# Reversed quarters, a least-loaded order for the values, sketches that add up in PSUM, and a new task list

## The chip, the cores and the metric

The kernel runs on one core of a Trainium2 chip. The metric is the device time of the program in microseconds. A core has five engines with a queue each: TensorE (PE), VectorE (DVE), ScalarE (ACT), GpSimd (POOL) and SyncE (SP), which here issues nearly all DMAs. Each works through its own instructions in order and waits on semaphores for the others.

## The reference

Two blocks follow each other. Shapes: batch 4, heads 4, sequence 1088, head size 32; in the second block width 128, 4 experts of size 64, 2 chosen for each row.

```python
def phi(x):                      # x: q or k
    a = einsum('rd,bhsd->bhsr', S1, x)
    b = einsum('rd,bhsd->bhsr', S2, x)
    return einsum('bhsi,bhsj->bhsij', a, b).reshape(..., 64)
kv  = einsum('bhsf,bhsd->bhfd', phi(k), v);   z = sum(phi(k), axis=2)
x   = (phi(q) @ kv) / (phi(q) @ z + 1e-6)     # heads side by side: (4, 1088, 128)

logits = x @ w_gate;  topk = the 2 largest of 4;  w = softmax over them
for e in range(4):
    q, k, v = x @ wq[e], x @ wk[e], x @ wv[e]
    a  = causal softmax(q @ k.T / sqrt(64))
    out += (e is chosen) * w[e] * (a @ v @ wo[e])
```

S1 and S2 come as 64-bit floats; the kernel splits them into two 32-bit parts, a high and a low one (`NS = 2`). All matmuls that count here are in 32-bit floats, and each shows as two passes in the trace.

## The kernel before, in words

The four batches go through the same stages, one batch shifted against the next. A list of words in the source, `ORDER`, is the program: `1.ks:4:9` calls the task `ks` for batch 1 with the arguments 4 and 9, and every engine's queue gets its instructions in the order of the words. Nothing is scheduled by itself; a word stands in all the queues that it uses.

A batch has 1088 rows, which are 9 tiles of 128 (the last has 64). The words of a batch are:

- `ld` loads k, q and v (SP). `bk`, `bq` (`bq0`, `bq1` by halves for batch 0) turn k and q on VectorE (L319 to L326). `vk` brings the first batch's v into place.
- `ks`, `qs`: `sketch` (L333). Matmuls with SKW, the arranged S, give a and b for some tiles (L345), with the high and the low part of S side by side; ScalarE copies one (L350), VectorE adds the other (L352), and a product of a and b makes the 64 features (L355), on VectorE for batch 0, on GpSimd for the others.
- `kv` (L368) multiplies k's features and v; `tf` turns q's features (L280, copied by L281), `nu` forms numerators and denominators (L384) and divides (L388 to L391), giving `xs`; `tx` turns `xs` into `xT`. `sp` spreads `xs` to `xrep` by 16 DMAs (L271), which has one buffer.
- `em` and `eo` make the experts' matrices `mcat` (query and key weights multiplied) and `mo` (value and output weights).
- `ga`, `ge`, `gw`: the gate, a chain of small operations. `mp` (batch 0) and `md` make masks from it, `mk`, by matmuls and casts (L491, L494) or by a round trip of DMAs through DRAM (L475 to L482).
- `cu:i` (`chosen`): x times mcat for the tiles i and i+1 (L502). The two chosen experts' results are picked by the masks (L509) into `uT`.
- `s:i:j` (`scores`): scores of a tile against all keys up to it, for both chosen experts (L542, L563 for tile 8). VectorE adds the causal mask and takes the maximum (L517), ScalarE the exponentials with their sums (L521).
- `t:i` turns a tile's weights in blocks of 32 by 32 (L264). Tiles 1 to 5 are group B, tiles 0, 6, 7, 8 group A.
- `vb:p`, `va:p`: `values` (L575), in four parts for each group. The sums over keys run by chunks c of 32 keys. Each of the four quarters r of 32 partitions holds the queries 32r to 32r+31 of every tile of the group, has its own 32 rows of the array and its own PSUM bank, and needs the chunks up to c = 4i + r of tile i. So quarter 3 needs the most. The loops go over c and inside it over r (L585, L587), with one matmul for all the units (tile and chosen expert) that still need c:

```python
        last = {(i, r): min(4 * i + r, NC - 1) for i in tiles for r in range(4)}
        for c in range(*PARTS[grp][part : part + 2]):
            for r in range(4):
                us = [x for x, (i, s) in enumerate(units) if c <= last[i, r]]
```

- `shb`, `sha`, `shp`: the gate's weights over the sums, spread over partitions. `zb` multiplies them in and sorts the units by expert (L665 to L668). `o` multiplies by mo (L675), copies (L678, two buffers `ob`) and writes the output (L680).
- `warm:n` issues n matmuls that nobody reads.

PSUM has eight banks; a task takes the least recently used ones, and the value sums hold four banks for the time of their group.

Of the kernel before, what the change touches and what calls it, by code (L numbers as in the profile page):

```python
# [10 lines left out]
F32 = mybir.dt.float32  # L11
BF16 = mybir.dt.bfloat16
U8 = mybir.dt.uint8
F8 = mybir.dt.float8e4
I32 = mybir.dt.int32
ALU = mybir.AluOpType
# [6 lines left out]
    0.bk 0.ks:4:9 0.warm:2 0.bq1 0.ks:0:4 0.vk 0.kv 0.bq0 0.qs:0:4 0.qs:4:9 1.ld 1.bk 0.warm:2 0.tf:0:8 0.warm:2  # L23
    0.nu:0:4 0.tf:8:13 0.tf:13:18 1.ks:4:9 0.tx:0:4 1.ks:0:4 0.nu:4:9 0.ga:0:4 0.em 0.mp:2:4 0.ge:0 0.mp:0:2 1.bq
    0.tx:4:9 2.ld 0.cu:2 0.gw:0 1.kv 1.qs:4:9 0.ga:4:9 0.sp 1.qs:0:4 0.cu:0 0.eo 1.tf:8:13 0.mp:8:9 0.md 0.mp:6:8
    0.mp:4:6 1.tf:13:18 2.bk 0.s:3 0.t:3 0.cu:4 0.cu:6 0.cu:8 2.bq 3.ld 1.tf:0:8 2.ks:0:4 0.s:5:1 1.nu:0:5 2.ks:4:9
    0.t:5 0.s:4:2 0.t:1 1.nu:5:9 0.s:6:0 2.kv 1.tx:4:9 0.ge:4 1.tx:0:4 0.t:4 0.t:2 0.s:8 0.gw:4 0.shb 2.qs:0:4 0.vb:0
    0.vb:1 0.t:0 0.t:8 1.ga:0:9 1.ge:0 1.md 0.t:6 0.s:7 0.vb:2 0.vb:3 0.t:7 1.cu:0 2.qs:4:9 1.cu:6 1.cu:2 0.sha 1.cu:4
    0.va:0 0.zb:1 2.tf:0:8 3.bq 1.gw:0 0.va:1 0.va:2 3.bk 2.tf:8:13 0.va:3 0.zb:6 1.sp 2.tf:13:18 3.ks:4:9 1.s:5:1
    0.o:6 1.cu:8 1.t:1 1.t:5 0.o:1 0.zb:3 1.s:4:2 0.zb:0 1.t:2 0.o:3 2.nu:5:9 3.ks:0:4 2.nu:0:5 1.s:3 1.shb 0.zb:5  # L30
    0.o:0 2.tx:4:9 1.s:7 2.tx:0:4 3.kv 1.t:3 1.t:4 0.zb:8 3.qs:4:9 1.s:6:0 1.vb:0 2.ga:0:9 1.s:8 2.md 1.vb:1 1.t:7
    0.o:8 1.t:8 1.t:6 1.vb:2 2.ge:0 1.vb:3 2.gw:0 2.cu:4 3.tf:13:18 2.cu:8 2.cu:0 1.t:0 0.o:5 2.cu:2 2.s:5:1 3.tf:8:13
    2.t:5 1.sha 2.s:4:2 2.t:2 1.zb:3 1.va:0 1.va:1 1.va:2 3.qs:0:4 1.va:3 1.o:3 1.zb:6 2.t:1 1.zb:1 2.sp 2.cu:6
    3.tf:0:8 2.s:3 1.o:6 1.o:1 2.t:3 2.t:4 2.s:7 1.zb:0 2.s:6:0 3.nu:5:9 3.nu:0:5 2.t:6 1.zb:8 2.vb:0 2.shb 3.tx:4:9
    1.o:0 3.tx:0:4 1.zb:5 2.t:7 2.vb:1 1.o:8 3.ga:0:9 3.ge:0 3.md 2.t:0 2.vb:2 2.vb:3 2.zb:1 1.o:5 2.s:8 2.t:8 3.cu:6
    2.o:1 2.sha 3.cu:4 3.cu:0 3.cu:8 3.cu:2 3.s:5:1 3.t:1 3.s:4:2 3.t:2 3.s:3 2.va:0 2.va:1 2.zb:3 3.gw:0 3.t:5 3.t:3
    2.va:2 2.va:3 3.sp 3.t:4 2.zb:6 2.o:3 3.s:7 3.s:6:0 2.zb:0 3.s:8 2.o:6 2.o:0 3.vb:0 2.zb:5 2.o:5 2.zb:8 3.t:8
    3.shb 3.t:6 3.t:0 3.vb:1 3.vb:2 3.t:7 3.vb:3 3.va:0 3.va:1 3.shp 3.zb:3 3.va:2 2.o:8 3.zb:1 3.va:3 3.o:3 3.zb:6
    3.o:1 3.o:6 3.zb:8 3.o:8 3.zb:5 3.o:5 3.zb:0 3.o:0
# [4 lines left out]
def kernel(  # L44
# [35 lines left out]
    def const(name, shape, dt=F32):  # L80
        return cp.tile(shape, dt, name=name, tag=name)
# [46 lines left out]
    S_sum = const("S_sum", [32, NS, 32])  # L128
    raw = S_sum.rearrange("p n d -> p (n d)") if NS == 1 else const("S_raw", [32, 32, 2], I32)
# [38 lines left out]
    nc.gpsimd.tensor_copy(identb, ident)  # L168
    nc.gpsimd.memset(SKW, 0.0)
# [5 lines left out]
    mask = const("mask", [128, 1024], BF16)  # L175
    mask_last = const("mask_last", [128, 64], BF16)
    nc.gpsimd.memset(mask, 0.0)
    nc.gpsimd.memset(mask_last, 0.0)
    for out_, cols in ((mask[:, 896:], 128), (mask_last[0:64], 64), (mask_last[64:], 64)):
        nc.gpsimd.affine_select(out=out_, in_=out_, compare_op=ALU.is_ge, fill=-1e30,  # L180
                                base=0, pattern=[[-1, cols]], channel_multiplier=1)
    lower = const("lower", [128, E, E])
    nc.gpsimd.memset(lower, 0.0)
    for e in range(1, E):
        nc.gpsimd.memset(lower[:, e, 0:e], 1.0)

    if NS == 2:
# [15 lines left out]
        def both(o, x, y, op):  # L203
            nc.vector.tensor_tensor(out=o, in0=x, in1=y, op=op)

        each(ex, hi, 20, SHR, 0x7FF, AND)
        each(ok, ex, 896, ALU.is_gt)
        each(ex, ex, 896, ALU.subtract, 0, ALU.max)
        each(ex, ex, 255, ALU.min)
        each(ex, ex, 23, SHL)  # L210
        each(sg, hi, 31, SHR, 31, SHL)
        both(sg, sg, ex, OR)
        each(ma, hi, 0xFFFFF, AND, 3, SHL)
        each(lw, lo, 29, SHR)
        both(ma, ma, lw, OR)
        both(ma, ma, sg, OR)
        both(lead, ma.bitcast(F32), ok, ALU.mult)
        each(lw, lo, 0x1FFFFFFF, AND)
        nc.vector.tensor_copy(last, lw)
        nc.vector.scalar_tensor_tensor(  # L220
            out=last, in0=last, scalar=2.0**-52, in1=sg.bitcast(F32), op0=ALU.mult, op1=ALU.mult)
        both(S_hi, lead, last, ALU.add)
# [3 lines left out]
    ST = const("ST", [32, NS, 32])  # L226
# [105 lines left out]

    def sketch(b, nm, j0, j1, eng):  # L333
        m_, xT_ = batch(b), {"k": kT, "q": qT}[nm]
# [80 lines left out]
    def gate(b, j0, j1):  # L415
        m_, k0 = batch(b), bank()
        for j in range(j0, j1):
            for r in range(4):
                x = 128 * j + 32 * r
                nc.tensor.matmul(P[32 * r : 32 * r + 32, k0, E * j : E * j + E], m_.xT[:, x : x + 32], wg,  # L420
                                 start=True, stop=True)
# [74 lines left out]
    def chosen(b, i):  # L496
# [30 lines left out]
    def step(b, tiles):  # L527
# [8 lines left out]
        for s in range(2):  # L536
# [8 lines left out]
            for x, i in enumerate(tiles):  # L545
                n = 128 * i + 128
                cols = slice(at[i], at[i] + n)
                m = mx[:, s, x : x + 1]
                take(a[:, s, cols], flat[:, f + at[i] : f + at[i] + n], mask[:, 1024 - n :], m)
                soften(a[:, s, cols], m, sum_of(m_, i, s))  # L550
# [24 lines left out]
    def values(b, grp, part):  # L575
# [8 lines left out]
        last = {(i, r): min(4 * i + r, NC - 1) for i in tiles for r in range(4)}  # L584
        for c in range(*PARTS[grp][part : part + 2]):  # L585
            (c0, _, u0), t = next((p, t) for p, t in zip(parts(grp), aT[grp]) if p[0] <= c < p[1])
            for r in range(4):  # L587
                us = [x for x, (i, s) in enumerate(units) if c <= last[i, r]]
                if us:
                    assert us[-1] == len(units) - 1  # L590
                    rows = slice(32 * r, 32 * r + 32)
                    nc.tensor.matmul(P[:, sums[grp][r], 32 * us[0] : 32 * len(units)],  # L592
                                     xrep[rows, c], t[rows, c - c0, us[0] - u0 :],
                                     start=(c == 0), stop=(c == max(last[i, r] for i in tiles)), skip_group_check=True)
# [54 lines left out]
    class Out:  # L649
# [21 lines left out]
        def put(self, copy=None):  # L671
# [7 lines left out]
            for t, i in enumerate(self.tiles):  # L679
                nc.sync.dma_start(out=out[self.b, 128 * i : 128 * i + nq, :], in_=ob[0:nq, t])  # L680
# [77 lines left out]
```

## Time and profile before

| | |
|---|---|
| runs before | 302.63 us median of 3, 299.61 to 303.94 |
| profiled execution | 301.3 us, span 299.5 us, mean granted clock 0.972 |
| TensorE busy | 280.1 us, 94% of the span |
| VectorE, ScalarE, GpSimd busy | 225.3, 106.6, 52.8 us |
| scores (L542) on PE | 66.2 us, 192 records |
| values (L592) on PE | 40.8 us (A) and 39.4 us (B), 1800 records |
| DMA moved | 26.04 MB, mean 87 GB/s |

A PE record is one pass of a matmul, and several quarters can be busy at once, so a group's busy time is the time in which any of them ran. The span goes from the first to the last instruction of the program; the profiled execution's own time is 1.8 us longer.

### The profile page before, as it was taken

How to read it: one execution, taken by the hardware profiler on the slowest of the kernel's cores; microseconds unless marked ns; L12 is line 12 of the kernel's file. 1: busy time of each engine (PE TensorE's matmuls, PEld its weight loads, DVE VectorE, ACT ScalarE, POOL GpSimd, SP SyncE). 2: the span in 40 equal slices, each digit the busy share in tenths (PEclk: the TensorE clock that was granted, in tenths of full speed). 3: DMA queues.
4: the chain of work that ended last, by engine and by line, in shares of the span. 5: the costliest groups of instructions: out<-in, count | busy, mean ns of one | idle time of the engine just before them, and what ended most of it. 6: DMA issues, size and time to landing. Idle time of an engine off the chain costs nothing.

```text
span 299.5 us, 10515 instructions
## 1 busy us (share of the span) xinstructions
PE 280.1 (94%) x4517; PEld 219.4 (73%) x4517; DVE 225.3 (75%) x507; ACT 106.6 (36%) x270; POOL 52.8 (18%) x129
## 2 busy tenths in 40 slices
PE   6397779999999899999999999999999999999996
PEld 2286667766768698786678679758877588489995
DVE  6837767799868679797785875989675788986462
ACT  2215514754705122345623162355124350450101
POOL 5005225023050314111321012000301001000200
PEclk9959597999999999999999999999999999999999
DMA  6752098380021224820203001482214102842001
GB/s 211 158 153 77 9 217 187 58 244 13 3 92 37 84 66 109 183 65 19 84 2 123 11 3 63 106 183 68 92 23 138 62 2 48 184 117 99 2 25 57
DMA packets 35846, 26.04 MB, mean 87 GB/s; under 512 B 9432, under 2 KB 33496, under 8 KB 35800
## 3 DMA queue, kind: packets, MB, share of 16 engines
q1 hardware_dynamic: 35784, 25.38, 32.6%
q8 instruction: 35, 0.57, 0.8%
q14 instruction: 11, 0.09, 0.1%
q10 hardware_dynamic: 16, 0.00, 0.0%
HBM read 14.16 MB, written 2.29 MB: 55 GB/s over the span
## 4 chain that ended last, share of the span: by engine, by line
PE 41%; DVE 13%; ACT 2%; DMA 2%; issue 2%; SPq 1%; POOL 1%; DVEq 0%; POOLq 0%; ACTq 0%
PE P L592 16%; PE P L542 12%; PE P L675 7%; PE P L502 2%; DVE uT L509 2%; ACT a L521 2%; DVE a L517 2%; DVE zT L668 2%; DMA mk<-dm 2%; DVE aTA L264 1%; SPq L475 1%; DVE zT L666 1%; PE P L563 1%; DVE aTB L264 1%; DVE xs L391 1%
## 5 line engine op out<-in xcount | busy, mean ns | idle before, releaser
L521 ACT ACTIVATE a<-a,mx 128x512 f32<-128x512 f32 (+8 forms) x68 | 53.8, 792 | 63.4 <-DVE mx L517 61.9
L542 PE MATMUL P<-xT,uT 128*128 128x512 f32 (+3 forms) x192 | 66.2, 494 | 0.6 <-DVE uT L509 0.6
L542 PEld LDWEIGHTS P<-xT,uT 128*128 128x128 f32 x192 | 33.1, 190 | 26.6 <-issue 19.1
L517 DVE CUSTOM_DVE_ANT_0 a<-P,mask 128x768 f32<-128x768 f32 (+4 forms) x64 | 44.8, 746 | 1.3 <-PE P L542 1.3
L592 PE MATMUL P<-aTA,xrep 32*128 32x160 f32 (+3 forms) x1080 | 40.8, 297 | 0.1
L592 PEld LDWEIGHTS P<-aTA,xrep 32*128 32x128 f32 x1080 | 38.8, 185 | 2.6 <-issue 0.9
L592 PE MATMUL P<-aTB,xrep 32*128 32x320 f32 (+4 forms) x720 | 39.4, 350 | 0.0
L502 PE MATMUL P<-xT,mcat 128*128 128x256 f32 (+1 forms) x160 | 36.6, 380 | 1.8 <-DVE uT L509 1.2
L675 PEld LDWEIGHTS P<-mo,zT 128*128 128x128 f32 (+1 forms) x288 | 33.9, 185 | 5.1 <-issue 2.7
L675 PE MATMUL P<-mo,zT 128*128 128x128 f32 (+1 forms) x288 | 37.0, 280 | 0.2 <-DVE zT L668 0.2
L592 PEld LDWEIGHTS P<-aTB,xrep 32*128 32x128 f32 x720 | 33.9, 185 | 4.2 <-issue 1.7
L509 DVE COPY_PREDICATED uT<-mk,P 128x512 f32<-128x512 uint8 (+1 forms) x40 | 24.7, 638 | 15.6 <-DMA mk<-dm 5.5
L502 PEld LDWEIGHTS P<-xT,mcat 128*128 128x128 f32 x160 | 29.0, 201 | 7.4 <-DVE uT L509 1.6
L264 DVE STREAM_TRANSPOSE aTB<-a 128x1024 f32<-128x1024 f32 (+3 forms) x28 | 24.7, 917 | 7.2 <-ACT a L521 7.1
L264 DVE STREAM_TRANSPOSE aTA<-a 128x256 f32<-128x256 f32 (+4 forms) x28 | 24.3, 915 | 1.4 <-ACT a L521 1.4
L666 DVE TENSOR_TENSOR zT<-yT,mk 128x768 f32<-128x768 f32 (+2 forms) x24 | 16.9, 704 | 5.4 <-PE P L675 5.3
L668 DVE COPY_PREDICATED zT<-mk,yT 128x768 f32<-128x768 uint8 (+2 forms) x24 | 18.6, 774 | 3.0 <-POOL zT L665 0.6
L678 ACT COPY ob<-P 128x256 f32<-128x256 f32 (+2 forms) x24 | 7.5, 313 | 34.6 <-PE P L675 25.9
L355 POOL TENSOR_TENSOR qp<-qab 128x1280 f32<-128x1280 f32 (+1 forms) x6 | 13.0, 2172 | 31.5 <-DVE qab L352 31.5
L355 POOL TENSOR_TENSOR kp<-kab 128x1280 f32<-128x1280 f32 (+1 forms) x6 | 13.0, 2172 | 31.7 <-DVE kab L352 21.9
L281 ACT COPY qpT<-P 128x640 f32<-128x640 f32 (+1 forms) x12 | 9.5, 804 | 17.7 <-PE P L280 17.7
L505 ACT COPY uT<-P 128x512 f32<-128x512 f32 (+1 forms) x20 | 10.5, 523 | 13.8 <-PE P L502 13.8
(179 smaller groups left out, 281.4 us busy)
## 6 DMA issues: line engine op xcount, KB each, us to landing
xrep<-xs SPq DMA_DIRECT2D x32, 144.0 KB
xrep<-xs SPq DMA_DIRECT2D x32, 128.0 KB
mk<-dm SPq DMA_DIRECT2D x3, 864.0 KB
kin<-in_k_dram SPq DMA_DIRECT2D x4, 544.0 KB
qin<-in_q_dram SPq DMA_DIRECT2D x4, 544.0 KB
vin<-in_v_dram SPq DMA_DIRECT2D x16, 128.0 KB
out_dram<-ob SPq DMA_DIRECT2D x32, 64.0 KB
sbc0B<-ds0B SPq DMA_DIRECT2D x1, 640.0 KB
```

The lines of the kernel that those rows point to most:

```text
L264: nc.vector.transpose(t[:, 0 : c1 - c0, n - u0 : n - u0 + s].rearrange("p c s k -> p s c k"), a[:, :, 32 * c0 : 32 * c1].rearrange("p s (c ...
L355: eng.tensor_tensor(out=fp[:, j0:j1].rearrange("p j h (x y) -> p (j h) x y", y=R), in0=a_[:, 1, :, None, :].to_broadcast([128, n, R, R]), ...
L502: nc.tensor.matmul(P[:, k0 + x // 2, x % 2 * w : x % 2 * w + w], mcat[:, e], m_.xT[:, 128 * i : 128 * i + w], start=True, stop=True)
L505: nc.scalar.copy(u.rearrange("p t s q -> p s t q"), P[:, k0, 0 : 2 * w].rearrange("p (s t q) -> p s t q", s=2, t=n))
L509: nc.vector.copy_predicated(u, mk[:, :, :, x].bitcast(U8), c[:, :, None].to_broadcast([128, n, 2, q]))
L517: nc.vector.tensor_tensor_reduce(out=dst, in0=src, in1=msk, scale=-1.0, scalar=most, op0=ALU.add, op1=ALU.min, accum_out=mx)
L521: nc.scalar.activation(out=a, in_=a, func=ACTF.Exp, bias=mx, scale=-1.0, accum_out=z)
L542: nc.tensor.matmul(flat[:, f + c : f + c + n], turned(b, i)[:, s], m_.xT[:, c - at[i] : c - at[i] + n], start=True, stop=True)
L592: nc.tensor.matmul(P[:, sums[grp][r], 32 * us[0] : 32 * len(units)], xrep[rows, c], t[rows, c - c0, us[0] - u0 :], start=(c == 0), stop=(c ...
L666: nc.vector.tensor_tensor(out=z[:, :, 0:X], in0=y[:, :, 0, None].to_broadcast([128, n, X, nq]), in1=mk[:, :, 0:X], op=ALU.mult)
L668: nc.vector.copy_predicated(z[:, :, 1:], mk[:, :, X:].bitcast(U8), y[:, :, 1, None].to_broadcast([128, n, X, nq]))
L675: nc.tensor.matmul(P[0:nq, k0, DM * t : DM * t + DM], self.zT[:, t, e], mo[:, e], start=(e == 0), stop=(e == E - 1))
```

## The change

1. For the tiles 0 to 3 (`BACK`) the four quarters of queries are held in reverse order: quarter r holds the queries 32(3-r) to 32(3-r)+31. So the gate, `chosen`, the mask of the scores (`mask_back`, added on the diagonal tile) and the output write follow that order. The write of such a tile is four DMAs of 32 rows, not one of 128.
2. `values` no longer goes by c and r. Each quarter has a list of its chunks, and the next matmul is always one of the quarter with the least work so far, a matmul counting as its columns, at least 128.
3. Batch 0's sketches have a function of their own. High and low part are two matmuls into the same PSUM words, so the adds fall away; the product reads one factor from PSUM. The features of its q lie in a buffer of the value weights.
4. The operations that split S are interleaved; its small tiles share one buffer. The masks are made ahead of the clearing of SKW, kT, qT and vp on GpSimd.
5. `ORDER` is a new list of the same 262 words.

```diff
 ORDER = """
-    0.bk 0.ks:4:9 0.warm:2 0.bq1 0.ks:0:4 0.vk 0.kv 0.bq0 0.qs:0:4 0.qs:4:9 1.ld 1.bk 0.warm:2 0.tf:0:8 0.warm:2
-    0.nu:0:4 0.tf:8:13 0.tf:13:18 1.ks:4:9 0.tx:0:4 1.ks:0:4 0.nu:4:9 0.ga:0:4 0.em 0.mp:2:4 0.ge:0 0.mp:0:2 1.bq
-    0.tx:4:9 2.ld 0.cu:2 0.gw:0 1.kv 1.qs:4:9 0.ga:4:9 0.sp 1.qs:0:4 0.cu:0 0.eo 1.tf:8:13 0.mp:8:9 0.md 0.mp:6:8
-    0.mp:4:6 1.tf:13:18 2.bk 0.s:3 0.t:3 0.cu:4 0.cu:6 0.cu:8 2.bq 3.ld 1.tf:0:8 2.ks:0:4 0.s:5:1 1.nu:0:5 2.ks:4:9
...
-    3.o:1 3.o:6 3.zb:8 3.o:8 3.zb:5 3.o:5 3.zb:0 3.o:0
+    0.bk 0.bq1 0.bq0 0.ks:4:9 0.ks:0:4 0.warm:2 0.qs:0:4 0.warm:2 0.vk 1.ld 0.qs:4:9 0.kv 1.bk 0.tf:0:8 0.warm:2 0.em
+    0.nu:0:4 1.ks:0:4 1.bq 0.tf:13:18 0.tf:8:13 0.tx:0:4 1.ks:4:9 0.nu:4:9 0.eo 0.tx:4:9 0.ga:0:4 0.ge:0 0.gw:0
+    0.ga:4:9 1.kv 0.mp:8:9 0.mp:2:4 2.ld 0.ge:4 0.mp:0:2 0.mp:6:8 0.mp:4:6 0.gw:4 2.bk 0.cu:2 1.qs:0:4 1.qs:4:9 0.cu:6
+    0.md 0.cu:4 0.cu:0 0.cu:8 1.tf:0:8 1.tf:8:13 0.s:5:1 0.s:3 0.t:1 1.tf:13:18 0.t:5 2.ks:4:9 0.sp 2.ks:0:4 0.s:4:2
+    0.s:7 1.nu:5:9 1.nu:0:5 0.shb 0.t:3 2.kv 1.tx:4:9 0.t:4 1.tx:0:4 0.s:8 0.t:2 0.t:7 1.ga:0:9 1.md 0.s:6:0 1.ge:0
...
+    3.o:6 3.zb:0 3.zb:5 3.o:0 3.o:5 3.zb:8 3.o:8
 """
...
+    BACK = (0, 1, 2, 3)
+    mask_back = const("mask_back", [128, 512], BF16)
...
+    def first_sketch(nm, j0, j1, eng):
...
+                    for n in range(NS):
+                        o = P[half : half + 64, k0 + m, 0 : 2 * w].rearrange("p (x d) -> p x d", x=2)
+                        nc.tensor.matmul(o[:, :, 2 * R * (j - j0) : 2 * R * (j - j0) + 2 * R], xT_[rows, x : x + 64],
+                                         SKW[rows, n].rearrange("p x h r -> p x (h r)"), start=(n == 0), stop=(n == NS - 1))
+        for m in range(2):
...
+            nc.scalar.copy(a, t[:, 0])
+            eng.tensor_tensor(
+                out=o, op=ALU.mult,
+                in0=t[:, 1].rearrange("p (j h) r -> p j h r", h=2)[:, :, :, None, :].to_broadcast([128, n, 2, R, R]),
+                in1=a.rearrange("p (j h) r -> p j h r", h=2)[:, :, :, :, None].to_broadcast([128, n, 2, R, R]))
...
-                x = 128 * j + 32 * r
+                x = 128 * j + 32 * (3 - r if j in BACK else r)
...
+        queries = m_.xT[:, 128 * i : 128 * i + w]
+        if i in BACK:
+            queries = queries.rearrange("p (t a q) -> p t a q", t=n, a=4)[:, :, ::-1]
...
-        last = {(i, r): min(4 * i + r, NC - 1) for i in tiles for r in range(4)}
-        for c in range(*PARTS[grp][part : part + 2]):
+        last = {(i, r): min(4 * i + (3 - r if i in BACK else r), NC - 1) for i in tiles for r in range(4)}
+        todo = {r: collections.deque(c for c in range(*PARTS[grp][part : part + 2]) if c <= max(last[i, r] for i in tiles))
+                for r in range(4)}
+        time = [0] * 4
+        while any(todo.values()):
+
+            r = min((r for r in range(4) if todo[r]), key=lambda r: time[r])
+            c = todo[r].popleft()
...
+            us = [x for x, (i, s) in enumerate(units) if c <= last[i, r]]
+            assert us == list(range(us[0], len(units)))
+            time[r] += max(32 * len(us), 128)
...
-                nc.sync.dma_start(out=out[self.b, 128 * i : 128 * i + nq, :], in_=ob[0:nq, t])
+                rows = out[self.b, 128 * i : 128 * i + nq, :]
+                if i in BACK:
+                    for r in range(4):
+                        nc.sync.dma_start(out=rows[96 - 32 * r : 128 - 32 * r], in_=ob[32 * r : 32 * r + 32, t])
+                else:
+                    nc.sync.dma_start(out=rows, in_=ob[0:nq, t])
```

The rest of the new list reads, from `1.ge:0` on:

```
    2.bq 0.vb:0 0.vb:1 0.vb:2 0.vb:3 0.zb:5 2.qs:4:9 2.qs:0:4 0.t:0 1.cu:2 0.t:8 0.o:5 1.cu:6 1.cu:4 1.cu:8 0.t:6
    1.cu:0 1.s:4:2 3.ld 3.bk 1.s:5:1 0.sha 0.va:0 0.va:1 1.t:5 2.tf:8:13 2.tf:13:18 0.va:2 1.gw:0 1.t:1 0.zb:3 0.va:3
    ...
    2.va:2 2.va:3 2.zb:0 3.s:3 3.sp 3.s:6:0 3.t:0 3.t:3 2.o:3 3.s:7 2.zb:8 3.gw:0 3.shb 2.o:0 3.s:8 2.o:8 3.t:6 3.vb:0
    3.t:8 3.vb:1 3.t:7 3.vb:2 3.vb:3 3.zb:1 3.va:0 3.va:1 3.va:2 3.o:1 3.zb:3 3.shp 2.zb:6 3.va:3 3.o:3 2.o:6 3.zb:6
    3.o:6 3.zb:0 3.zb:5 3.o:0 3.o:5 3.zb:8 3.o:8
```

## The prediction

> **What bounds the kernel now.** I read the busy shares, then the clock row of the 40 slices, then the busy time by stretches, then TensorE's rows of the timeline.
>
> ```profile
> PE 280.1 (94%) x4517; PEld 219.4 (73%) x4517; DVE 225.3 (75%) x507; ACT 106.6 (36%) x270; POOL 52.8 (18%) x129
> PEclk9959597999999999999999999999999999999999
> ```
>
> TensorE is busy for 94% of the span, and its clock is at half only in the first six slices. The stretches say where the missing 6% lies:
>
> ```profile
> 0.00:60.00 60.00, 46.39 (x893) 36.06 (x894) 40.69 (x108) 23.50 (x58) 16.08 (x33) 0.86 0.55 134
> 60.00:100.00 40.00, 40.00 (x682) 28.95 (x680) 32.95 (x83) 17.85 (x49) 8.88 (x15) 1.00 0.29 88
> 140.00:180.00 40.00, 39.63 (x588) 29.97 (x588) 30.25 (x72) 16.36 (x42) 6.12 (x18) 1.00 0.14 45
> ```
>
> The columns are stretch, length, busy TensorE, weight loads, VectorE, ScalarE, GpSimd, then granted clock. TensorE lacks 13.6 us in the first 60 us and works part of them at half clock; later it lacks almost nothing. So there are two kernels in one: a start-up set by a chain of waits over all engines, and from about 52 us on a queue of matmuls whose sum is the time. VectorE is second, at about 80%.
>
> ```profile
> 14.66 4.06 PE L368 MATMUL P<-vp,kp 128*64 128x33 f32 x72 [4.09 <-DVE kp L355]
> 39.14 2.29 PE L368 MATMUL P<-vp,kp 128*64 128x33 f32 x72
> 59.70 3.71 PE L542 MATMUL P<-xT,uT 128*128 128x512 f32 x12
> 154.66 5.04 PE L592 MATMUL P<-aTB,xrep 32*128 32x256 f32 x116
> 241.34 9.63 PE L592 MATMUL P<-aTA,xrep 32*128 32x224 f32 x270
> ```
>
> (Start, length, group.) The same 72 matmuls of kvs take 4.06 us behind a wait and 2.29 us in the full-clock queue. The row at 59.70 is `0.s:5:1`. I take that word as the seam: it is in both lists, with all of the first batch's `cu` ahead of it. The PE rows of the words behind it, each at its full-clock price (kv 2.2, cu 1.86, a 1024-column s 3.65, o of a pair 1.9, values 19 a batch), add up to 233.7 us. 59.7 + 233.7 = 293.4 against the last matmul's end at 296.6: only 3.3 us are lost behind the seam. The sum of the new kernel is (start of `0.s:5:1`) + (PE work behind it) + (losses) + (end).
>
> **Part 1, values.** Each quarter of 32 rows of the array runs its own matmuls beside the others. In the records of L592 a quarter starts the next pass after 269 ns at 320 columns, 215 at 256, 163 at 192, 136 at 160, and 111 at 128, 64 and 32 alike. So a pass costs 0.84 ns a column with a floor at 128 columns, each matmul has two passes, and a run of parts lasts as long as its fullest quarter. Summed over a batch, quarters r = 0 to 3 carry in B 7.5, 8.1, 8.6, 9.15 us and in A 8.7, 9.1, 9.2, 9.37. The trace agrees: A in one run is 9.56 long (chain of waits), B's last two parts 4.97 where quarter 3 sums to 4.82; 0.15 to 0.19 is the run's start. With tiles 0 to 3 reversed the same work stands as B 8.5, 8.4, 8.3, 8.2 and A 9.0, 9.2, 9.1, 9.05. With all parts in one run that is 0.67 + 0.2 us a batch. Parts cut off by other matmuls end each with their own fullest quarter, so I add up the runs as the new list cuts them: batch 0 saves 1.05 (fewer cuts too), 1 0.6, 2 0.4, 3 1.05: **3.1 us**. If quarters had to be fed strictly in the program's order of c, the reversal would gain nothing, as every c has a full quarter; the least-loaded order is then what makes it work, so I keep 3.1, with ends 0 and 3.5. The queries read in reversed blocks of 32 in L502, and the gate's and masks' other slices, keep their element counts: 0, at most 0.1 us on each of 16 groups.
>
> **Part 2, sketches of batch 0.** Instead of 36 matmuls of 64 columns for k (1.4 us with two passes), 72 of 32 columns. Row L384, 33 columns on the same 64*64 tiles, takes 1.14 us for 64 records, 17 ns each as with 64 columns (L345: 40 in 0.81). So PE pays 2.5 instead of 1.4 for k and again for q: +2.2 us, where it is idle. VectorE loses the adds (0.56 + 0.47 twice) and its products now read PSUM: two of 640 and two of 512 elements. The nearest row is L599 with 820 ns for 640 from PSUM: 1.6 + 1.3 us, where add and product took 2.05 + 1.7 for k. Gain 0.8 for each of k and q, ends 0 and 1.2.
>
> **Part 3, start-up, step by step** (before from the timeline; after = producers' ends plus durations of the same rows):
> - S split (L199 to L227): 18 operations, 0.2 us apart where each needs the last, 0.09 where not. Interleaved, 2.3 instead of 3.3 us: turned S at 5.7 (6.7).
> - GpSimd now makes the masks first (0.9 + 0.5 + 0.15 us memsets, about 1.9 selects, 0.3 `lower`), so SKW is cleared at 5.6 and its last copy ends at 6.45 (7.18): most of that gain stays, 0.3 is given up.
> - k turned 7.9 (8.57); q turned next in VectorE's queue, 10.3 (15.6); k features 13.1 (14.5); q features **16.0 (24.5)**. Before, `0.kv` stood ahead of `0.qs` in PE's queue, waited for k's product and ran at half clock until 18.7. Now qs fills that wait and kv ends at 16.2.
> - Behind it `em` (1.6 us) fits while ScalarE copies qpT; first numerators end 20.7 (24.9); xs, tx, second numerators at 25; xT whole 28.1 (37.3).
> - Both halves of the gate then run back to back on VectorE, 2.2 + 2.3 + 2.2 us: sel whole at 34.6 (47.0). In the old trace one L436 took 2.31 us beside a GpSimd product; the new place has none.
> - 36 mask matmuls, and nine casts of 0.53 on ScalarE: mk whole at 40 (54).
> - PE then has `cu` x5 (8.4), qs (1.4), tf (1.1): about 50. PE is nearly idle from 31 to 35.
>
> On that idle time a rule is weighed. In the trace the clock is 0.5 from 14.2 to 21.0, 31.3 to 38.1 and 44.9 to 48.3, the first of these after an idle stretch from 10.6 to 14.7, and cu took 2.79 and 3.54 us there, 1.9 later. The Trainium skill, "TensorE: Matmul & The Clock Gate", The HAM clock gate, says that one idle window of some 3.4 us halves the clock until a busy one has passed. By the row alone, new gaps being shorter, I would add 0; by the rule the gap at 31 costs one slow stretch, 3.4 us at half, 1.7 us. I take 1.5, hence **51.5** for `0.s:5:1`, ends 48.5 and 57.
>
> **Part 4, behind the seam.** 0.s:3, 2.ks:0:4 and 1.tf:13:18 (1.8 + 0.65 + 0.45) now stand behind it: 233.7 + 2.9 - 3.1 = 233.5. Losses: 3.3 as before, plus VectorE. Adding VectorE's rows by word from the seam, its sum is at most 0.6 us ahead of PE's in the old list; in the new it is 2.8 ahead at `0.vb:0` and 0.5 at `1.s:6:0`. Such a lead stops PE: +1.5, ends 0 and 6. Loads and xrep: `2.nu` comes 16 us of PE work after `0.va:3`, where one xrep round takes about 13; `3.vb:0` 15.0 us after `2.va:3` (14.1 before): no wait.
>
> **Output DMAs.** Tiles 0 to 3 go out in four pieces: 48 more issues. L680 holds SP's queue 0.43 us each, 20 us over the kernel. Queued behind them are shares, masks, loads and xrep. The rule against it: "DMA: Bandwidth & Descriptors", Rules for kernel authors, wants small transfers coalesced, with a fixed cost of some 2 us each (Anatomy of one DMA, for the GpSimd path). By the rule as busy time this is 48 x 2 = 96 us; by the row 20 us of a queue that waits longer than that (37.7 us on ob alone). I take the row, so 0 except at the end: `3.o:0` issues four (1.7 us), and `3.o:8` needs the same one of two ob buffers, as one ob copy already waits for a DMA in the old tail. Landing about 1.4 us after the last issue: **+1.2 us**.
>
> **Sum.** 51.5 + 233.5 + 3.3 + 1.5 + 1.2 = 291.0 for the last matmul and its copy's wait (before 296.6); with the same 2.9 us to the span's end 293.9, and 1.8 outside it (301.3 - 299.5): **295.7 us**. The profiled execution lies 1.3 below the median 302.63 of the runs; I leave it so.
>
> **Rivals.**
> 1. *The start-up gain gets stuck* (27%): another slow clock stretch, or GpSimd's k product holding VectorE's gate as L436 was held, puts the seam at 57: 5.5 more, 301.2. For: three slow stretches before. Against: q features need neither.
> 2. *VectorE becomes the bound* (9%, slower). Place: `0.s:5:1` to `2.tx`, where its sum stays within 3 us of PE's (before up to 6 us of slack). It decides once its own waits in that stretch exceed about 10% of it. With 12 us lost there instead of 1.5: 306.2. Against: PE stayed full over this stretch before with VectorE at 82%.
> 3. *The reversal gains nothing* (10%): a quarter's turn keeps the queue in order after all: 298.8.
> My forecast's own case has 54%.
>
> About 2% is what a measurement can tell here. Faster by more needs under 296.6: most of my case and little of the rest, 0.57; within 2% 0.34; slower 0.09. The range, 289 to 303, takes the seam from 48.5 and the rivals up to the second.
>
> **What would show it.** Right: full TensorE slices from about 40 us on, `0.s:5:1` near 51, q product ended near 16, L592's counterpart near 75 us of chained time instead of 78, PE idle under 6 us behind the seam. Wrong: PE waits "<-DVE" in 60 to 150 us; a slow clock past 42 us; A or B runs as long as before; ScalarE's last ob copy waiting more than 2 us on out_dram.

## The result, and the profile after

| | before | after |
|---|---|---|
| median of the runs | 302.49 us of 4 (299.61 to 303.94) | 292.63 us of 4 (291.85 to 296.24) |
| profiled execution, span | 301.3, 299.5 us | 293.26, 291.4 us |
| TensorE busy, mean granted clock | 280.1 us, 0.972 | 269.9 us, 0.982 |
| start of `0.s:5:1` (the seam) | 59.70 us | 48.81 us |
| from there to the last matmul's end | 236.9 us | 238.0 us |
| from there to the span's end | 2.90 us | 4.51 us |

The ratio is 0.968, with a 95% interval of 0.958 to 0.977. The same kernel measured a second time gave 0.977 (0.970 to 0.984), so a difference of 1% between two variants below is not told apart by their times alone. Executions that a disturbance had lengthened are in the medians and left out of the ratios.

The gain is at the start: the seam comes 10.9 us earlier. Behind it the kernel is 1.1 us longer to the last matmul, and then 1.6 us longer to the end.

The busy shares and the clock row of the page after:

```profile
PE 269.9 (93%) x4661; PEld 215.9 (74%) x4661; DVE 220.6 (76%) x503; ACT 105.9 (36%) x270; POOL 53.6 (18%) x134
PEclk9999889997799999999999999999999999999999
```

TensorE does 10.2 us less, but the share of 93% is where it was. The clock row has two dips, one in the start-up (slices 5 and 6) and one behind the seam (slices 10 and 11), where the old row was full. The busy time by stretches (stretch, length, busy TensorE, weight loads, VectorE, ScalarE, GpSimd, granted clock, DMA share, GB/s):

```profile
0.00:52.00 52.00, 42.55 (x1001) 34.13 (x1002) 35.53 (x112) 21.35 (x55) 17.34 (x40) 0.97 0.41 110
52.00:100.00 48.00, 43.85 (x740) 32.37 (x739) 36.43 (x85) 20.82 (x55) 10.96 (x15) 0.93 0.47 117
180.00:220.00 40.00, 40.00 (x613) 31.18 (x609) 31.50 (x66) 15.39 (x36) 3.66 (x14) 1.00 0.40 106
```

The start-up lacks 9.5 us of TensorE in 52, where 13.6 were lacking in 60. But the stretch from 52 to 100 us lacks 4.2 us and runs at 0.93, in a part of the kernel that lost nothing before. TensorE's rows say where (start, length, group, idle time before it):

```profile
14.48 1.70 PE L406 MATMUL P<-vp,kp 128*64 128x33 f32 x50
16.82 0.83 PE L406 MATMUL P<-vp,kp 128*64 128x33 f32 x22 [0.63 <-issue]
71.57 1.23 PE L287 MATMUL P<-ident,xs 64*128 64x64 f32 x18 [4.13 <-DVE xs L429]
72.72 3.59 PE L604 MATMUL P<-xT,uT 128*64 128x64 f32 x12
171.41 9.41 PE L638 MATMUL P<-aTA,xrep 32*128 32x224 f32 x270
```

`kv` no longer waits for the features of k: its 72 matmuls take 1.70 + 0.83 us where they took 4.06, and the wait of 4.09 ahead of them is gone. A whole run of group A takes 9.41 us instead of 9.63. The third row is the one that the forecast did not have: before `1.tx`, TensorE stands still for 4.13 us. It names VectorE; VectorE's own row names a DMA, and SyncE's queue and the chain of waits name the cause (VectorE's row, SyncE's rows, one piece of the chain):

```profile
69.44 0.76 DVE L429 TENSOR_TENSOR xs<-P,den 128x256 f32<-128x256 f32 x2 [4.80 <-DMA xrep<-xs]
```

```profile
45.67 3.58 SPq L513 DMA_DIRECT2D dm<-sel  x8
51.87 1.03 SPq L519 DMA_DIRECT2D mk<-dm  x2
52.94 13.13 SPq L278 DMA_DIRECT2D xrep<-xs  x16
```

```profile
65.45 3.90 DMA xrep<-xs
```

`1.nu` writes `xs`, which `0.sp` still reads: the 16 DMAs that spread batch 0's `xs` over `xrep`. In SyncE's queue they stand behind the DMAs of `0.md`, whose second pair waits for the first to land, so they are issued only from 52.9 to 66.1 us, and the last lands at 69.35. The pause lasts from 67.4 to 71.6 us. From 69.05 us, within it, to 75.9 the clock is at half; the scores of tile 8 at 72.72 take 3.59 us in it.

The end, in SyncE's and ScalarE's rows:

```profile
284.96 1.96 SPq L728 DMA_DIRECT2D out_dram<-ob  x4
```

```profile
288.25 0.26 ACT L723 COPY ob<-P 64x128 f32<-64x128 f32 x1 [1.85 <-DMA out_dram<-ob]
```

The four writes of `3.o:0` hold the queue 1.96 us, and the copy of the last tile waits 1.85 us for one of the two output buffers. The row that answers to it before waited 0.65 us for TensorE (`before`):

```profile
296.69 0.27 ACT L678 COPY ob<-P 128x128 f32<-128x128 f32 x1 [0.65 <-PE P L675]
```

### The profile page after: what moved, and what is told of

It reads as the page before. It is cut to its first block, busy times and chain, and to the rows that moved or that the text cites. A ratio compares the mean times of both kernels' runs of the same rounds, so it can differ in the third digit from the quotient of the medians.

```text
span 291.4 us, 10880 instructions
## 1 busy us (share of the span) xinstructions
PE 269.9 (93%) x4661; PEld 215.9 (74%) x4661; DVE 220.6 (76%) x503; ACT 105.9 (36%) x270; POOL 53.6 (18%) x134
## 4 chain that ended last, share of the span: by engine, by line
PE 71%; DVE 12%; SPq 5%; DMA 5%; issue 3%; POOL 1%; ACT 1%; DVEq 0%; ACTq 0%; POOLq 0%
PE P L638 22%; PE P L582 18%; PE P L720 9%; PE P L543 9%; SPq L278 4%; PE P L604 3%; PE P L287 2%; PE P L422 2%; DVE aTA L271 2%; PE P L356 2%; DMA mk<-dm 2%; DVE uT L549 1%; DVE qT L332 1%; DVE xs L429 1%; DMA xrep<-xs 1%
## 5 line engine op out<-in xcount | busy, mean ns | idle before, releaser
L561 ACT ACTIVATE a<-a,mx 128x128 f32<-128x128 f32 (+7 forms) x68 | 53.7, 791 | 67.5 <-DVE mx L557 67.2
L582 PEld LDWEIGHTS P<-xT,uT 128*128 128x128 f32 x192 | 33.5, 190 | 27.5 <-issue 20.7
L638 PE MATMUL P<-aTA,xrep 32*128 32x160 f32 (+3 forms) x1080 | 38.7, 295 | 0.0
L638 PE MATMUL P<-aTB,xrep 32*128 32x320 f32 (+4 forms) x720 | 37.4, 348 | 0.0
L720 PEld LDWEIGHTS P<-mo,zT 128*128 128x128 f32 (+1 forms) x288 | 33.9, 186 | 3.8 <-issue 1.7
L557 DVE CUSTOM_DVE_ANT_0 a<-P,mask 128x768 f32<-128x768 f32 (+3 forms) x32 | 32.2, 1014 | 4.0 <-PE P L582 4.0
L543 PE MATMUL P<-xT,mcat 128*128 128x256 f32 (+1 forms) x160 | 33.3, 361 | 0.7 <-DVE uT L549 0.7
L543 PEld LDWEIGHTS P<-xT,mcat 128*128 128x128 f32 x160 | 27.6, 191 | 4.3 <-DVE uT L549 1.1
L723 ACT COPY ob<-P 128x256 f32<-128x256 f32 (+2 forms) x24 | 7.5, 311 | 34.6 <-PE P L720 17.0
L393 POOL TENSOR_TENSOR kp<-kab 128x1024 f32<-128x1024 f32 (+1 forms) x6 | 12.9, 2171 | 25.1 <-DVE kab L390 24.6
L393 POOL TENSOR_TENSOR qp<-qab 128x1024 f32<-128x1024 f32 (+1 forms) x6 | 12.9, 2170 | 15.2 <-DVE qab L390 15.2
L710 POOL MEMSET zT<- 128x256 f32 (+2 forms) x24 | 5.7, 249 | 53.9 <-PE P L720 45.6
L557 DVE CUSTOM_DVE_ANT_0 a<-P,mask_back 128x256 f32<-128x256 f32 (+3 forms) x32 | 15.1, 485 | 0.0
```

The costliest lines, as they stand in the source:

```text
L393: eng.tensor_tensor(out=fp[:, j0:j1].rearrange("p j h (x y) -> p (j h) x y", y=R), in0=a_[:, 1, :, None, :].to_broadcast([128, n, R, R]), ...
L557: nc.vector.tensor_tensor_reduce(out=dst, in0=src, in1=msk, scale=-1.0, scalar=most, op0=ALU.add, op1=ALU.min, accum_out=mx)
L561: nc.scalar.activation(out=a, in_=a, func=ACTF.Exp, bias=mx, scale=-1.0, accum_out=z)
L582: nc.tensor.matmul(flat[:, f + c : f + c + n], turned(b, i)[:, s], m_.xT[:, c - at[i] : c - at[i] + n], start=True, stop=True)
L720: nc.tensor.matmul(P[0:nq, k0, DM * t : DM * t + DM], self.zT[:, t, e], mo[:, e], start=(e == 0), stop=(e == E - 1))
```

## The experiments

Each variant's ratio is to the kernel before, run on the same chip beside it. "Behind" is the time from the seam to the last matmul's end, "tail" the rest of the span, "values" the time of the value matmuls on TensorE, each record counted to the start of the next, so that waits inside a run are in it; all are from the profiled execution.

| | median us | ratio, interval | seam | behind | tail | values |
|---|---|---|---|---|---|---|
| before | 302.49 | | 59.70 | 236.9 | 2.90 | 78.4 |
| after | 292.63 | 0.968 (0.958 to 0.977) | 48.81 | 238.0 | 4.51 | 74.6 |
| `after_again` | 294.74 | 0.977 (0.970 to 0.984) | 49.51 | 239.2 | 4.53 | 74.7 |
| `new_code_old_list` | 307.43 | 1.021 (1.015 to 1.028) | 60.78 | 237.4 | 6.71 | 78.4 |
| `old_code_new_list` | 301.42 | 1.000 (0.997 to 1.003) | 55.02 | 241.5 | 3.19 | 76.4 |
| `shared_features` | 298.24 | 0.989 (0.982 to 0.996) | 53.05 | 238.3 | 4.69 | 74.6 |
| `adds_on_vector` | 293.21 | 0.976 (0.966 to 0.986) | 47.95 | 237.2 | 4.72 | 74.6 |
| `no_reversal` | 294.01 | 0.975 (0.971 to 0.980) | 50.19 | 238.9 | 3.18 | 76.7 |
| `by_chunk` | 295.16 | 0.982 (0.976 to 0.989) | 49.62 | 239.1 | 4.56 | 75.1 |
| `spread_early` | 287.96 | 0.956 (0.948 to 0.963) | 48.51 | 232.0 | 5.02 | 74.6 |
| `late_ob` | 294.07 | 0.964 (0.953 to 0.974) | 54.25 | 237.5 | 3.43 | 74.8 |
| `both` | 289.42 | 0.959 (0.953 to 0.965) | 52.46 | 232.2 | 3.40 | 74.6 |
| `kept_warm` | 294.86 | 0.973 (0.963 to 0.984) | 50.20 | 238.1 | 4.53 | 76.3 |

The values of `kept_warm` have the code of the changed kernel; 1.7 us more came from two of its 13 runs of value matmuls (3.27 and 5.39 us, where the changed kernel has 2.42 and 4.50). The other eleven agree to 0.01 us in both, so the values are compared below run by run.

### The list or the code

Two kernels take one part each: all the new code with the old list (the edit below), and the old code with the new list (its reverse).

```diff
 ORDER = """
-    0.bk 0.bq1 0.bq0 0.ks:4:9 0.ks:0:4 0.warm:2 0.qs:0:4 0.warm:2 0.vk 1.ld 0.qs:4:9 0.kv 1.bk 0.tf:0:8 0.warm:2 0.em
...
+    0.bk 0.ks:4:9 0.warm:2 0.bq1 0.ks:0:4 0.vk 0.kv 0.bq0 0.qs:0:4 0.qs:4:9 1.ld 1.bk 0.warm:2 0.tf:0:8 0.warm:2
...
 """
```

> The new code with the old list of words. Theory (start-up by order, values by code): the q features stay behind kv as before, so 0.s:5:1 starts at 57 to 60 us; value runs sum to about 75 us of chained time as in the new kernel (78.4 before); no 4.1 us stop at 1.tx. Span about 299.5 - 3.7 (values) - 0 to 2 (sketches) + 1.5 (four-piece writes at the end) = 295 to 297, time 297 to 299. Rival (the code makes the gain, the list is neutral): 0.s:5:1 at 50 to 53 and a time of 293 to 295.

> The old code with the new list. Theory: the list alone moves the start-up: q features ready at 17 to 19 us (16.4 in the new kernel, 24.5 before), 0.s:5:1 at 49.5 to 52; the stop of PE at 1.tx is there with 3 to 5 us, since 0.sp stands behind 0.md in both; value runs sum to about 78. Span 291.4 + 3.7 + 1 to 2 - 1.5 = 294.5 to 295.5, time about 296.5. Rival (the list needs the code): 0.s:5:1 after 55 and a time above 300.

Neither part alone is faster. The code under the old list is 2.1% slower, where 297 to 299 us had been expected; the list with the old code brings nothing, where 296.5 us had been expected and its rival ("the list needs the code") named over 300. Together they bring 3.2%, or 2.3% when measured again. So the parts are not a sum.

With the old list, `0.kv` still stands ahead of `0.qs` on TensorE, and the features of q end at 22.0 us: 2.5 us earlier than before, but 5.7 later than with both parts (TensorE's, VectorE's, ScalarE's and SyncE's rows of `new_code_old_list`):

```profile
12.91 3.64 PE L406 MATMUL P<-vp,kp 128*64 128x33 f32 x72 [1.90 <-DVE kp L364]
```

```profile
18.07 1.29 DVE L364 TENSOR_TENSOR aTB<-P,ab 128x512 f32<-128x512 f32 x2 [3.62 <-ACT ab L363]
```

```profile
298.55 0.26 ACT L723 COPY ob<-P 64x128 f32<-64x128 f32 x1 [3.28 <-DMA out_dram<-ob]
```

```profile
301.04 1.72 SPq L728 DMA_DIRECT2D out_dram<-ob  x4
```

k's product gained (the wait ahead of `kv` is 1.90 instead of 4.09 us), but q's waits behind it, and what was gained is lost again ahead of the seam, where the clock is at half from 47.6 to 54.4 us. The values gain nothing either: 78.4 us, where 75 had been expected. TensorE's busy time in them is about 1.3 us less than before, and the waits inside the runs of value matmuls are as much more. The loss is mostly at the end: the old list ends with `3.o:0`, whose four writes come last of all, and the copies wait for the output buffers. The tail is 3.8 us longer than before.

With the new list and the old code, q's sketches are early, but their product is not (VectorE's rows of `old_code_new_list`):

```profile
14.64 0.49 DVE L352 TENSOR_TENSOR qab<-P,qab 128x128 f32<-128x128 f32 x2 [0.39 <-ACT qab L350]
18.79 1.23 DVE L355 TENSOR_TENSOR qp<-qab 128x1024 f32<-128x1024 f32 x1 [3.67 <-PE P L368]
```

The factors are there at 15.1 us, and the product waits 3.67 us for `kv` (L368): the features of q lie in the buffer of k's features, which `kv` has to have read. `kv` itself is late here too, since it waits for the copy of v, `0.vk`, on ScalarE:

```profile
15.79 2.97 PE L368 MATMUL P<-vp,kp 128*64 128x33 f32 x72 [3.07 <-ACT vp L693]
```

The features of q end at 22.0 us, and the seam is at 55.02, still 4.7 us earlier than before. Behind it the kernel is 4.6 us longer than before, so nothing is left of that. Part 3 of the change, the features of q in a buffer of the value weights, takes the first of these waits away.

### The features' own buffer alone

To test that by one edit, the changed kernel with q's features put back:

```diff
-            m_.fp[nm] = (p2.tile([128, NJ, H, R * R], F32, tag="fp", name="kp0", bufs=1) if nm == "k" else
-                         aT["B"][0].rearrange("p c u k -> p (c u k)")[:, 0 : NJ * H * R * R]
-                         .rearrange("p (j h f) -> p j h f", j=NJ, h=H))
+            m_.fp[nm] = p2.tile([128, NJ, H, R * R], F32, tag="fp", name=f"{nm}p0", bufs=1)
```

> The new kernel with one thing undone: the features of the first batch's q go back into the buffer that also holds k's features, which kv reads. Theory (the buffer of its own is what lets the new list work): the first q product waits for kv on PE and starts at 17.5 to 19 us (12.5 in the new kernel), 0.s:5:1 starts at 52.5 to 55 (48.8), time 296 to 299. Rival (the sums in PSUM and the interleaved split make the start-up gain): 0.s:5:1 within 1 us of the new kernel's, time 292 to 294.

It came to 298.24 us, as expected: the one line gives back about half of the gain. VectorE's row shows the wait (`shared_features`):

```profile
18.28 2.75 DVE L362 TENSOR_TENSOR qp<-P,ab 128x512 f32<-128x512 f32 x4 [5.68 <-PE P L404]
```

The features end at 21.0 instead of 16.4 us. Not all of the 4.2 us at the seam is this wait itself. In this execution the clock is at half from 18.3 to 28.6 us. `both` and `late_ob`, below, have their features on time but the same stretch of half clock (from 17.8 and 17.65 us, 10.24 us long), and their seams are at 52.46 and 54.25, about as late. In both, TensorE had stood inside `kv`, after 50 of its 72 records, with nothing that the profile shows it to wait for; in the changed kernel it stood there for 0.63 us (`both`, then `late_ob`):

```profile
17.64 1.29 PE L406 MATMUL P<-vp,kp 128*64 128x33 f32 x22 [1.18 <-issue]
```

```profile
18.18 1.39 PE L406 MATMUL P<-vp,kp 128*64 128x33 f32 x22 [2.55 <-issue]
```

All four executions of `shared_features` have a mean clock of 0.958 to 0.963, against 0.961 to 0.982 in eight of the changed kernel. So the wait shows in the trace and its cost in the times; how much of that cost is the wait and how much is half clock that comes with it, I could not separate. The half of the gain that stays has not been divided either: the interleaved split of S and the earlier masks (part 4) were never undone alone.

### The sums in PSUM

The sketches of before, with their adds on VectorE, but q's factors and features still in a buffer of their own:

```diff
-        if b == 0:
-            return first_sketch(nm, j0, j1, eng)
...
+            if (b, nm) == (0, "q"):
+                free, n0 = aT["B"][0].rearrange("p c u k -> p (c u k)"), NJ * H * R * R
+                m_.fp[nm] = free[:, 0:n0].rearrange("p (j h f) -> p j h f", j=NJ, h=H)
...
```

> The new kernel with the first batch's sketches as before (high and low part side by side, added by VectorE), but k and q keep buffers of their own. Theory: the adds cost VectorE 0.8 us for each of k and q, and PE saves 2.2 us where it waits; 0.s:5:1 starts 0.5 to 2 us later than in the new kernel, time 293 to 295. Rival (sums in PSUM carry the start-up gain): 3 us later or more, 296 to 298.

293.21 us, and a seam of 47.95 us, 0.9 earlier than in the changed kernel where 0.5 to 2 later had been expected: sums in PSUM bring nothing that shows. TensorE's rows of `adds_on_vector`, then of the changed kernel:

```profile
7.91 1.28 PE L386 MATMUL P<-SKW,kT 64*64 64x64 f32 x72 [1.62 <-DVE kT L328]
13.72 2.29 PE L409 MATMUL P<-vp,kp 128*64 128x33 f32 x72 [1.68 <-DVE kp L396]
```

```profile
7.92 2.35 PE L356 MATMUL P<-SKW,kT 64*64 64x32 f32 x144 [1.59 <-DVE kT L328]
```

144 records of 32 columns take 2.35 us, 72 of 64 take 1.28: what VectorE saves on adds, TensorE spends on sketches. With the adds, `kv` even ends first (16.0 against 17.65 us).

### Reversal and order of the values

```diff
-    BACK = (0, 1, 2, 3)
+    BACK = ()
```

> The new kernel with BACK empty: no tile is reversed, writes are single DMAs again, the least-loaded order stays. Theory (quarter 3 sets a run's length): value runs sum to 74.6 + 2.5 to 3.7 = 77 to 78.4 us, the end after the last matmul shrinks from 4.55 to about 2.9. Time 292.6 + 3 - 1.6 = 294 (293 to 295). Rival (the order makes the gain, not the balance): value runs stay at 74.6 to 75.5, time 291 to 292.

```diff
-            r = min((r for r in range(4) if todo[r]), key=lambda r: time[r])
-            c = todo[r].popleft()
+            c, r = min((todo[r][0], r) for r in range(4) if todo[r])
+            todo[r].popleft()
```

> The new kernel, but values issues by chunk and quarter as before; the quarters stay reversed. Theory A (a quarter's queue runs ahead of the others): value runs stay at 74.6 to 75.2 us, time within 0.5 us of the new kernel. Theory B (matmuls start strictly in the program's order, so each chunk lasts as long as its fullest quarter): runs 77.5 to 78.5 us, time 3 to 4 us above the new kernel, 296.

With `old_code_new_list` these give all four cases under the new list, in us of the values:

| | queries in order | tiles 0 to 3 reversed |
|---|---|---|
| by c, then r | 76.4 | 75.1 |
| least loaded quarter | 76.7 | 74.6 |

The reversal gives 1.3 us under the plain order, and 2.2 under the least loaded one (0.4 of it in the two runs named next). The order alone gives nothing: the 0.4 us more lie in two of the 13 runs (2.67 against 2.44 us, 4.71 against 4.55), of which the first takes 2.42 to 3.27 us from profile to profile of the same value code; the others agree to 0.02 us. On top of the reversal the order gives 0.5 us, in four runs, whose lengths in the balanced order repeat to 0.01 us from profile to profile. Two long runs show the reversal: batch 2's A in one run, and batch 3's last parts of B, to which A follows (TensorE's rows of `no_reversal`, of `by_chunk`, then of after):

```profile
234.34 9.57 PE L638 MATMUL P<-aTA,xrep 32*128 32x224 f32 x270
258.17 9.01 PE L638 MATMUL P<-aTB,xrep 32*128 32x320 f32 x177
```

```profile
234.58 9.41 PE L638 MATMUL P<-aTA,xrep 32*128 32x224 f32 x270
258.24 8.89 PE L638 MATMUL P<-aTB,xrep 32*128 32x320 f32 x176
```

```profile
232.81 9.41 PE L638 MATMUL P<-aTA,xrep 32*128 32x224 f32 x270
256.47 8.66 PE L638 MATMUL P<-aTB,xrep 32*128 32x320 f32 x176
```

A takes 9.41 us with the reversal in either order, 9.57 without. B takes 9.01, 8.89 and 8.66 us, of one record more or fewer. `by_chunk` took 295.16 us, 2.5 above the changed kernel's first median, where at most 0.5 had been expected, and 0.4 above its second. In time the reversal is not told apart from nothing: it saves 2.2 us of values and pays 1.3 of them back, since without it a tile is one write and the tail is 3.18 instead of 4.51 us.

### The stop before `1.tx`

```diff
-    ... 0.ga:4:9 1.kv 0.mp:8:9 0.mp:2:4 2.ld 0.ge:4 ... 2.ks:4:9 0.sp 2.ks:0:4 ...
+    ... 0.ga:4:9 1.kv 0.mp:8:9 0.mp:2:4 2.ld 0.sp 0.ge:4 ... 2.ks:4:9 2.ks:0:4 ...
```

> The new list with the word 0.sp moved up behind 2.ld, ahead of 0.md in SP's queue. Theory (the stop of PE at 1.tx comes from the first xrep round, which starts late behind the masks' DMAs and still reads xs when 1.nu wants to write it): the round runs at about 30 to 43 us, the 4.1 us stop and the slow clock stretch behind it go, 1.tx starts right behind 2.kv; 4 to 5.5 us less, time 287 to 289. Rival (VectorE is late there anyway): a stop of 2 us or more stays, time 290.5 to 292.6.

287.96 us, as expected, and the fastest kernel of the study: 4.7 us under the changed kernel's first median, and 0.956 (0.948 to 0.963) of the one before. SyncE's row, TensorE's rows and the clock row of `spread_early`:

```profile
29.89 12.51 SPq L278 DMA_DIRECT2D xrep<-xs  x16
45.37 3.59 SPq L513 DMA_DIRECT2D dm<-sel  x8
```

```profile
67.07 0.77 PE L287 MATMUL P<-ident,xs 64*128 64x64 f32 x18
67.77 2.05 PE L604 MATMUL P<-xT,uT 128*64 128x64 f32 x12
```

```profile
PEclk9999989999999999999999999999999999999998
```

The spread is now issued ahead of `0.md`, and the transposes have no wait in front of them. The dip in slices 10 and 11 has gone with the pause, and the scores of tile 8 are back at 2.05 us. Behind the seam the kernel is 6.0 us shorter, which is about the pause (4.13) and what the half clock had cost the words behind it (1.54 on L604 alone).

The other runs bear this out. In all nine profiles of the new list with `0.sp` in its place, half clock begins between 69 and 76 us; in `spread_early` and `both`, which move it, there is none there. In seven of the nine TensorE waits 3.4 to 4.1 us for `xs` ahead of `1.tx`. In the other two, `old_code_new_list` and `adds_on_vector`, VectorE waits 3.29 and 2.79 us for the same DMAs, but TensorE's pause (2.48 and 1.99 us) stands just before, inside `2.kv`, and the profile shows no cause for it.

### The output buffers at the end

Six places for the last batch's output tiles, in the buffers that held the last batch's q and k:

```diff
-            ob = p2.tile([128, 2, DM], F32, tag="ob", name=f"ob{self.nm}")
+            if self.b < B - 1:
+                ob = p2.tile([128, 2, DM], F32, tag="ob", name=f"ob{self.nm}")
+            else:
+                x = [1, 3, 6, 0, 5, 8].index(self.tiles[0])
+                ob = (kin, qin)[x // 4][:, 256 * (x % 4) : 256 * (x % 4) + 256].rearrange("p (t d) -> p t d", t=2)
```

> The new kernel with room for all six output tiles of the last batch (in the input tiles of k and q, which are dead by then) instead of two ob buffers in turn. Theory (the last ob copy waits 1.85 us for the four-piece write of 3.o:0): no ob copy waits for out_dram in the last batch, the last copy ends 0.4 us after the last matmul, the end after it shrinks from 4.5 to about 3.0 us; time 291.1, 1.5 less. Rival (the four issues on SP's queue hold the last write all the same): 4 us or more stay.

The tail is 3.43 instead of 4.51 us, and no copy waits for a DMA (ScalarE's and SyncE's last rows):

```profile
291.78 0.26 ACT L727 COPY qin<-P 64x128 f32<-64x128 f32 x1 [0.75 <-PE P L720]
```

```profile
289.81 1.95 SPq L732 DMA_DIRECT2D out_dram<-kin  x4
291.87 1.00 SPq L734 DMA_DIRECT2D out_dram<-qin  x2
```

The last two writes now stand directly behind the four of `3.o:0` in the queue. 291.1 us had been expected; the four executions took 290.07, 291.07, 297.07 and 299.07 us, at mean clocks of 0.970, 0.962, 0.952 and 0.943. The profiled one is the third of these, and its seam, at 54.25, is 5.4 us later than in the changed kernel, though the two programs are the same up to the last batch's output. So the tail is compared here, and the time is not.

> The changed kernel with two edits together: the first batch's spread word 0.sp moved up behind 2.ld, and six own places for the last batch's output tiles, so that no copy of an output tile waits for an output DMA. If the two losses are separate (the stop before the transposes of xs at 67 us, the queue for output buffers at the end), the gains add: 288.0 for the first edit alone, 1 to 1.5 less for the second, 286.5 to 287, and the end after the last matmul falls from about 5 to about 3.4 us. If the output DMAs themselves set the end (issue and landing, whatever the buffers), the end keeps about 5 us and the time stays at 288.

Behind the seam and in the tail, `both` is what was expected: 232.2 and 3.40 us, against 232.0 and 5.02 of `spread_early` alone, 1.5 us less. Its time (289.42 us, where 286.5 to 287 had been expected) is not lower, since its start is later: seam 52.46 against 48.51 us. Its clock row:

```profile
PEclk9975979999999999999999999999999999999999
```

The clock is at half from 17.8 to 28.0 us, which `spread_early`'s row does not have, though the two programs are the same up to the last batch's output. So the edit of the buffers saves 1.5 us of the trace; in the times it is not told apart from nothing.

### The clock in the start-up

```diff
-    0.ga:4:9 1.kv 0.mp:8:9 ...
+    0.ga:4:9 1.kv 0.warm:16 0.mp:8:9 ...
```

> The changed kernel with 16 matmuls that nobody reads between 1.kv and 0.mp:8:9, in TensorE's idle time of 3.5 us before the mask matmuls. If that idle time causes the stretch of half clock behind it (34.9 to 38.3 us), the stretch goes, the mask matmuls (3.78 us) take about 2.5, and the seam comes up to 1.7 us earlier: 47.1 to 48.3, 291 us. If the casts on ScalarE set the pace of the masks anyway, the clock is full there but the seam stays at 48.8 and the time at 292.6. If a window of half clock isn't caused by the idle time before it, it stays where it is.

> The changed kernel once more, unchanged, to see how far its own time, seam and stretches of half clock move between measurements. If the half clock follows the waits of the program, the stretches stand again at 35 to 38 and 69 to 76 us; if they come by chance, they stand elsewhere. The ratio should lie within 0.01 of 0.968.

`kept_warm` did not answer its question. The clock was at half from 28.75 to 35.6 us, from before the idle time that was to be filled, and the 16 matmuls started in it (TensorE's rows):

```profile
33.35 4.71 PE L758 MATMUL P<-identb 128*128 128x512 bf16 x16
37.90 2.17 PE L529 MATMUL P<-identb,selb 128*128 128x128 bf16 x36
```

The masks' matmuls took 2.17 us instead of 3.78, but started at 37.90 instead of 34.95: the seam is at 50.20. `after_again` shows why one profile could not have settled it (its clock row):

```profile
PEclk9999579998799999999999999999999999999999
```

In the same program the start-up's half clock is from 29.5 to 39.8 us now, 10.24 us long, and was from 34.9 to 38.3 before. The one behind the pause at 67 us is in both. In `after_again` the long stretch cost the seam only 0.7 us: it slows `1.kv`, behind which TensorE waits for the selection until 34.95 in either case. The one from 17.8 us in `both` cost about 4, against `spread_early`.

## Why the prediction was right, and where it was not

The forecast was 295.7 us; 292.63 was measured, and 293.26 in the profiled execution, against which the sum is to be held. Its own case came true: the gain is in the start-up, and it comes in good part from the early features of q. By its steps:

- **The seam.** 51.5 forecast, 48.81 measured. This 2.7 us is more than all of the 2.4 by which the sum is too high; the other terms give 0.3 back. The chain of part 3 held step by step: k features 12.6 (13.1 forecast), q features 16.36 (16.0), first numerators 21.74 (20.7), sel whole 34.69 (34.6), `mk` whole 40.2 (40). But `cu` does not wait for the whole of `mk`: its first matmul starts at 38.56, behind those of the masks. The three groups that follow, 8.4 + 1.4 + 1.1 us, make 10.9 and not the 10 that I added; they took 10.25. The 1.5 us for the clock did not come on top: in this execution the stretch of half clock stood where the rule put it, at 34.9 us after 3.5 us of idle time, and fell on the masks' matmuls, which ended early all the same.
- **The clock rule.** That the stretch stood there is one case. In the repeated run it began at 29.5, after 3.41 us in which TensorE had been busy for 2.39, and in `both` at 17.8, after 2.23 us of busy time in 3.41. In `spread_early` 1.83 us of busy time (157.2 to 160.6 us) were followed by full clock. So one wholly idle window is not what it takes here, and TensorE's busy time does not sort the cases; what sets a stretch off stays open. (The first reading of the clock row is also off: its low slices are the third, fifth and seventh, as the times given later in the prediction have it.)
- **Why q's features are early.** Here the step that failed is the credit: "Before, `0.kv` stood ahead of `0.qs` in PE's queue". That is true and not enough. With the list alone the product waits 3.67 us for `kv`, for the buffer that q shared with k. The time was right because the change has both.
- **Sketches.** PE's +2.2 us and VectorE's saving were right in kind, and the whole part is worth nothing that shows: `adds_on_vector` has its seam 0.9 us earlier. I had `kv`'s end at 16.2; it is at 17.65 with the new sketches, 16.0 with the old.
- **Values.** -3.1 forecast, -3.9 measured (78.42 to 74.56), of which the list alone makes 2.1 and reversal and order 1.8. Under the old list the same reversal and order left the sum where it was. My condition, "if quarters had to be fed strictly in the program's order of c, the reversal would gain nothing", is refuted: by c and r it still gains 1.3 us. The third rival is thus wrong in its mechanism, not only in its size.
- **PE's work behind the seam.** 233.5 forecast, 230.5 measured, waits left out. For the three words moved there I had added 2.9 us; scores, sketches and transposes together grew by about 1 us, the half clock on L604 (about 1.5 us more) left out. `cu` and `o` are 2.3 us shorter than before, at the same counts. Most of this is `o`, and goes with the list: `o` takes 35.3 us under the old list and 33.9 under the new one, with either code. Why, no run shows.
- **Losses behind the seam.** 3.3 + 1.5 forecast, 7.5 measured, where "under 6 us" had been named as a sign of being right. The 1.5 was for VectorE's lead, and that did not stop TensorE. The stop was of a kind that the sum did not look for: I had followed `sp` to its next reader (`2.nu`, "no wait") but not to the next writer of `xs`, `1.nu`, nor `0.sp` past `0.md` in SyncE's queue. That is 4.13 us, and the half clock with it. It and the cheaper matmuls cancel: 238.3 was forecast for the whole from the seam to the last matmul, 238.0 came. That these two errors are of one size is luck.
- **The end.** +1.2 forecast, +1.6 measured, by the mechanism given: the copy of `3.o:8` waits 1.85 us.
- **The signs.** Two of those named for "wrong" did show: a wait "<-DVE" at 67 us and a slow clock past 42 us. Neither meant VectorE as the bound (second rival): VectorE was itself waiting for a DMA, and with that DMA moved both signs are gone. The first rival's seam of 57 did not come, though half clock from 17.7 us put it at 52.5 in `both` and 54.3 in `late_ob`.

## What to carry to other kernels

When a word is moved in a queue, check for each of its instructions not only who reads what it writes, but who next writes what it reads, and what it stands behind in the DMA queue: here that was 4.1 us of wait plus the clock after it, and one word moved 22 words up won it back. An operation can start early only if its output has a free place: the new list brought nothing with the old code, where q's features had no buffer of their own, and the new kernel without that buffer gave back about half of its gain. So list and code had to be tried together before either was judged. A wait at the end of the chain is read one engine further: TensorE's row named VectorE, VectorE's row named the DMA.

## What the runs showed of the hardware

- Quarters of the array run ahead of each other even when their matmuls are issued in turn. In `by_chunk`'s run of A at 234.58 us, chunk 1 is narrower for quarter 3 (160 columns) than for the others (224). Quarter 3 then starts chunk 2 at 235.35 and chunk 3 at 235.62, quarter 0 at 235.44 and 235.82, though in the program each of quarter 3's matmuls stands behind quarter 0's of the same chunk. The long run of A took the same 9.41 us by chunk and quarter as in the balanced order; all of the values differ by 0.5 us in 75.
- The start-up's half clock moved between executions of one program: one stretch of 3.41 us at 34.9, or 10.24 us at 29.5. Its lengths were multiples of 3.41 us in every profile here (3.41, 6.83, 10.24, 13.65, read to 0.01), outside the cut at the span's end. Where it fell decided its price, 0.7 or about 4 us of the same 10.24. That is the size of the differences between variants here, and a variant's profile was compared only after its clock row.
